# Attention and two mixtures of experts: late tokens of one expert chosen by a product with ones and zeros, list reads on another queue, gathers at another place

## The chip, the cores and the metric

The kernel runs on one core of one Trainium2 chip. The metric is the device time of one launch in microseconds: 1219.24 us is the median of 3 runs of the kernel before (1219.02 to 1221.35).

## The reference

Three layers follow each other. The first is causal attention with a decay, over 2 batches, 8 heads, 576 positions and 64 columns a head; its output is a matrix x of N = 1152 tokens by D = 512. The second is a mixture in which every token goes through all E = 8 experts (F = 1024), weighted by a matrix P that eight rounds of normalising make. The third sends each token to the two experts with its highest noisy logits. Cut to the last layer, which the change touches:

```python
def _moe2_ref(x, w_gate, w_noise, noise, w1, w2):
    noisy = x @ w_gate + np.log1p(np.exp(x @ w_noise)) * noise
    top2 = np.argpartition(-noisy, 2, axis=1)[:, :2]
    top2_w = softmax of the two values of each token
    for e in range(E):
        for k in range(2):
            mask = top2[:, k] == e
            h = np.maximum(x[mask] @ w1[e], 0.0)
            out[mask] += top2_w[mask, k, None] * (h @ w2[e])
```

## The kernel before

All large products are split: each f32 operand is stored as a high part and the rest (`xh` and `xl`, `w1h` and `w1l`, `hth` and `htl`), and three matmuls stand for one product. A step of a first product is L205 to L207, of a second product L641 to L643. Weights come from memory in pieces of 512 KB into four `raw` buffers (`load_w`, SyncE's queue, L180 for w1 and L183 for w2). `conv_w` turns a piece into its two parts, with a cast on ScalarE (L200) and a subtraction on VectorE (L201).

The first mixture works through units of 256 or 384 tokens. Its last two experts are ordered so that the first 896 tokens (early) are finished before the last 256 (late). While the late tokens are still in the first mixture, the early ones are already routed for the second. Routing ranks the eight logits of each token on VectorE (`route_rank`, `route_places`), finds for each of its two experts the next free place in that expert's list, and scatters (token number, weight) to `table_scratch` in memory (L969, GpSimd). A place is a row of the table; expert 0 has two lists, list 0 for early tokens and list 1 for late ones, and experts 1 to 7 make lists 2 to 8, worked through in the order of their lengths (`order_lists`, `by_length`, and `pick`, which loads an expert's number into a register of SyncE, L1018).

A list l goes through these steps. `read_list(l)` loads its part of the table into `tb` (L988, SyncE's queue) and makes clipped indices `ix` (L989, VectorE). `gather_x(l)` fetches the rows of x with one indirect DMA for each 128 places or fewer (L1030, GpSimd) into a part of `acc`, one of two halves by turns (`xsl[l % 2]`). `turn_x(l)` transposes them on TensorE (L1044) and makes `xh` and `xl` with a copy on ScalarE (L1046) and a subtraction on VectorE (L1047). `m2_g1(l)` is the first product and its ReLU. List 1 has its own form with the tokens as the fixed operand: L1058 to L1060, a ReLU on ScalarE (L1062), four transposes (L1065), and `hth` and `htl` from ScalarE (L1068) and VectorE (L1069). `m2_g2(l)` is the second product, with a gather of what `out` holds by now (L1076) for l above 1. The result is scaled and scattered to `out` (L1110 and L1113 on VectorE, L1114 on GpSimd). Its TensorE accumulators are the `y` buffers, of which there are three.

The passage from the first to the second mixture is written out in `last_units`. Each piece of work gets a planned time, the pieces are sorted by it, and called in that order. The pieces of `T_ROUTE`, `T_CONV` and `T_TURN` are offsets in us from the end of a second product; a step of a second product counts 3 x (512/2400 + 0.0026). `T_TURN` places `turn_x(0)` inside the second product of the unit `i0 + 4`. `early_done` reads and gathers list 0; `late_done`, after the late routing, orders the lists, loads the first weight piece, reads and gathers lists 1 and 2, picks lists 3 to 8 and loads three more pieces. After `last_units` come list 0's second product, list 1's turn and first product, the reads of lists 3 to 8, list 3's gather, list 2's turn, and then the loop over lists 2 to 8, in which list l + 1 is turned in the middle of list l's second product.

Outside blocks with a manual schedule the order of instructions on an engine need not be that of the source: a scheduler places each by its own estimate of readiness. Matmuls in `pin` keep their place behind what was traced before them on TensorE. Each engine then runs its queue in order.

Of the kernel before, what the change touches and what calls it, by code (L numbers as in the profile page):

```python
# [10 lines left out]
F32 = mybir.dt.float32  # L11
F32R = mybir.dt.float32r
BF = mybir.dt.bfloat16
I32 = mybir.dt.int32
# [39 lines left out]
T_ROUTE = [[1.45, 1.8, 3.0, 5.75, 11.65, 0.4, 4.2], [2.0, 3.7, 4.0, 5.9, 6.85, 2.15, 5.55], [1.05, 1.6, 2.65, 6.2, 7.4, 0.4, 3.9], [1.0, 1.15, 2.3, 5.4, 7.15, 3.5, 0.6]]  # L54

T_CONV = [[-1.1, 0.7], [-4.5, 1.65], [2.95, 4.35], [13.6, 2.75]]
T_TURN = 5.75

class Plan:

# [65 lines left out]
def attn_moe_moe2_kernel(ctx: ExitStack, tc: tile.TileContext, q, k, v, f, wg1, w1, w2,  # L126
# [702 lines left out]
    for l in range(E + 1):  # L829
        for t in range(extra[l]):  # L830
            nc.gpsimd.memset(limit[:, l, t:t + 1], float((base[l] if l == 1 else 0) + caps[l] + t * 128))
    number = mp.tile([1, E], F32, name="number")
    for e in range(E):
        nc.gpsimd.memset(number[:, e:e + 1], float(e))
# [105 lines left out]
    def route_places(t0, t1):  # L940
        n = t1 - t0
        rk, nl, kbf = RT.pop("rank")
        pr = RT.pop("pr")
        km = mp.tile([128, 2, 3, E], F32, name="r_km")[:, :, 0:n]
        for z in range(2):
            nc.vector.tensor_scalar(km[:, z], rk, float(z), None, op0=OP.is_equal)
        kw = mp.tile([128, 2, 3, E], F32, name="r_kw")[:, :, 0:n]
        m12 = mp.tile([128, 2, 3], F32, name="r_m12")[:, :, 0:n]
        nc.vector.tensor_tensor(kw, km, nl[:, None].to_broadcast([128, 2, n, E]), op=OP.mult)
        nc.vector.tensor_reduce(m12, kw, axis=AX.X, op=OP.add)  # L950
        ex = mp.tile([128, 3], F32, name="r_ex")[:, 0:n]
        nc.vector.tensor_tensor(ex, m12[:, 1], m12[:, 0], op=OP.subtract)
        nc.scalar.activation(ex, ex, AF.Exp)
        pos = mp.tile([128, 3, E], F32, name="r_pos")[:, 0:n]
        nc.vector.tensor_tensor(pos, pr[:, 0:n * E].rearrange("p (t e) -> p t e", e=E),
                                nxt[:, None, :].to_broadcast([128, n, E]), op=OP.add)
        nc.vector.tensor_tensor(nxt, nxt, pr[:, 64:64 + E], op=OP.add)
        nc.vector.tensor_tensor(kw, km, pos[:, None].to_broadcast([128, 2, n, E]), op=OP.mult)
        pf = mp.tile([128, 2, 3], F32, name="r_pf")[:, :, 0:n]
        nc.vector.tensor_reduce(pf, kw, axis=AX.X, op=OP.add)  # L960
        nc.vector.tensor_copy(place[:, :, t0:t1], pf)  # L961
        sm = mp.tile([128, 3], F32, name="r_sm")[:, 0:n]
        wr = rows.bitcast(F32)[:, t0:t1]
        nc.vector.tensor_scalar(sm, ex, 1.0, 1e-9, op0=OP.add, op1=OP.add)
        nc.vector.reciprocal(wr[:, :, 0, 1], sm)
        nc.vector.tensor_tensor(wr[:, :, 1, 1], ex, wr[:, :, 0, 1], op=OP.mult)
        for t in range(t0, t1):
            for z in range(2):
                s = nc.gpsimd.indirect_dma_start(  # L969
                    out=table, out_offset=bass.IndirectOffsetOnAxis(ap=place[:, z, t:t + 1], axis=0),  # L970
                    in_=rows[:, t, z, :], in_offset=None)
                for o in scat:
                    tc.declare_no_dep(s.ins, o.ins, reason="each list entry has one writer")
                scat.append(s)

    tabs, idxs = {}, {}

    def read_list(l):

        nt = -(-caps[l] // 128)  # L980
        st = caps[l] // nt
        tb = mp.tile([st, nt, 2], I32, name=f"tb{l}")
        ix = mp.tile([st, nt], I32, name=f"ix{l}")
        if l < 2:
            src = table[base[l]:base[l] + caps[l], :]
        else:
            src = table[ds(by_length[l - 2] * room + (base[2] - room), caps[l]), :]
        nc.sync.dma_start(tb, src.rearrange("(s t) c -> s t c", t=nt))  # L988
        nc.vector.tensor_scalar(ix, tb[:, :, 0], float((NT - TC if l == 0 else NT) - 1), None, op0=OP.min)  # L989
        tabs[l], idxs[l] = tb, ix  # L990

    def order_lists():

# [32 lines left out]
    def gather_x(l):  # L1026
        ix = idxs[l]
        st = ix.shape[0]
        for t in range(ix.shape[1]):
            nc.gpsimd.indirect_dma_start(  # L1030
                out=xsl[l % 2][0:st, t, :], out_offset=None, in_=x2d[0:NT - TC] if l == 0 else x2d,
                in_offset=bass.IndirectOffsetOnAxis(ap=ix[:, t:t + 1], axis=0))

    def cols(l):
        c = xcol[l % 2]
        return xh[:, :, c.start:c.start + caps[l]], xl[:, :, c.start:c.start + caps[l]]

    def turn_x(l):
        st, nt = idxs[l].shape
        ah, al = cols(l)  # L1040
        for kc in range(KC):
# [3 lines left out]
                                        ident[0:st, 0:st]))  # L1045
            nc.scalar.copy(ah[:, kc], pt[:, :caps[l]])  # L1046
            nc.vector.tensor_tensor(al[:, kc], pt[:, :caps[l]], ah[:, kc].bitcast(F32), op=OP.subtract)  # L1047

    def m2_g1(l, ht, fcs=range(FC)):
        ah, al = cols(l)  # L1050
# [79 lines left out]
    def last_units(i0):  # L1130
# [88 lines left out]
        def late_done():  # L1219
# [2 lines left out]
            pick(2)  # L1222
            load_w(E + 1, 0, (0,))
            read_list(1)
            gather_x(1)
            read_list(2)
            gather_x(2)
            for l in range(3, E + 1):
                pick(l)
            load_w(E + 1, 0, (1, 2, 3))  # L1230

        now = unit(0, i0 + 1)
        now, ends = back(now, i0)
# [25 lines left out]
    for i, (s, e, c0, n) in enumerate(units[:hi - 5]):  # L1259
# [7 lines left out]
        if units[i + 1][0] != s:  # L1267
            conv_next(s + 1, 1)
    last_units(hi - 5)
    m2_g2(0, hts[hi % 2])  # L1270
    turn_x(1)
    m2_g1(1, hts[(hi + 1) % 2])

    for l in range(3, E + 1):
        read_list(l)
    gather_x(3)
    turn_x(2)
    s = E + 1
    conv_next(s + 1, 0)
    m2_g2(1, hts[(hi + 1) % 2])  # L1280
    conv_next(s + 1, 1)
    for l in range(2, E + 1):
# [4 lines left out]
        m2_g1(l, ht, range(2, FC))  # L1287
        s = E + l
        if l < E:
            if l > 2:  # L1290
                gather_x(l + 1)
            conv_next(s + 1, 0)
        m2_g2(l, ht, (lambda: turn_x(l + 1)) if l < E else None)
        if l < E:
            conv_next(s + 1, 1)

# [83 lines left out]
```

## Time and profile before

| | |
|---|---|
| runs, median | 1219.24 us |
| profiled execution, time | 1218.53 us |
| its span, first to last instruction | 1216.5 us |
| mean granted TensorE clock | 0.991 |
| TensorE busy (matmul) | 1180.1 us, 97% |
| VectorE, ScalarE, GpSimd busy | 521.7, 381.3, 196.8 us |
| memory moved | 100.90 MB, mean 83 GB/s |

The span is what the trace shows; the time has some 2 us around it. TensorE's busy share is that of matmuls in flight. The granted clock is a share of 2.4 GHz; 0.50 is the level of 1.2 GHz. A wait in brackets is idle time of the engine ahead of the instruction, with the instruction or transfer that ended it.

### The profile page before, as it was taken

How to read it: one execution, taken by the hardware profiler on the slowest of the kernel's cores; microseconds unless marked ns; L12 is line 12 of the kernel's file. 1: busy time of each engine (PE TensorE's matmuls, PEld its weight loads, DVE VectorE, ACT ScalarE, POOL GpSimd, SP SyncE). 2: the span in 40 equal slices, each digit the busy share in tenths (PEclk: the TensorE clock that was granted, in tenths of full speed). 3: DMA queues.
4: the chain of work that ended last, by engine and by line, in shares of the span. 5: the costliest groups of instructions: out<-in, count | busy, mean ns of one | idle time of the engine just before them, and what ended most of it. 6: DMA issues, size and time to landing. Idle time of an engine off the chain costs nothing. (4 is left out here: it accounts for less than half of the span.)

```text
span 1216.5 us, 17348 instructions
## 1 busy us (share of the span) xinstructions
PE 1180.1 (97%) x6949; PEld 1090.1 (90%) x6949; DVE 521.7 (43%) x1042; ACT 381.3 (31%) x725; POOL 196.8 (16%) x273
## 2 busy tenths in 40 slices
PE   7999999999999999999999999999999969999996
PEld 6899989999999999999999999998897959999995
DVE  5887565232232332313323223223455646556541
ACT  4787522122121221212212112212133335444440
POOL 4854500000000000000000000000112143443232
PEclk9999999999999999999999999999999989999998
DMA  5541142021120201202102112012032368676632
GB/s 135 141 88 41 46 150 70 1 70 35 35 70 1 70 18 52 70 1 70 60 10 70 33 37 70 32 39 79 27 96 85 107 197 238 200 225 215 185 89 62
DMA packets 104041, 100.90 MB, mean 83 GB/s; under 512 B 44798, under 2 KB 79742, under 8 KB 103951
## 3 DMA queue, kind: packets, MB, share of 16 engines
q1 hardware_dynamic: 90799, 85.44, 23.2%
q0 software_dynamic: 13152, 14.27, 4.2%
q8 instruction: 56, 0.92, 0.3%
q14 instruction: 34, 0.28, 0.1%
HBM read 90.05 MB, written 9.98 MB: 82 GB/s over the span
## 5 line engine op out<-in xcount | busy, mean ns | idle before, releaser
L205 PE MATMUL h<-xh,w1h 128*128 128x384 f32 (+8 forms) x1056 | 336.4, 319 | 1.0 <-DVE htl L636 1.0
L207 PE MATMUL h<-xh,w1l 128*128 128x384 f32 (+8 forms) x1056 | 334.3, 317 | 0.0
L206 PE MATMUL h<-xl,w1h 128*128 128x384 f32 (+8 forms) x1056 | 334.2, 317 | 0.0
L635 ACT ACTIVATE hth<-h 128x384 fp32r<-128x384 f32 (+8 forms) x264 | 119.3, 454 | 477.8 <-PE h L207 477.7
L643 PE MATMUL y<-w2h,htl 128*128 128x512 f32 (+1 forms) x624 | 244.4, 392 | 8.1 <-DVE htl L1069 8.1
L641 PE MATMUL y<-w2h,hth 128*128 128x512 f32 (+1 forms) x624 | 244.9, 392 | 0.0
L642 PE MATMUL y<-w2l,hth 128*128 128x512 f32 (+1 forms) x624 | 244.1, 391 | 0.0
L636 DVE SCALAR_TENSOR_TENSOR htl<-h,hth 128x384 fp32r<-128x384 f32 (+8 forms) x264 | 132.7, 508 | 186.6 <-ACT hth L635 186.3
L205 PEld LDWEIGHTS h<-xh,w1h 128*128 128x128 f32 x1056 | 199.3, 189 | 2.9 <-DVE htl L636 1.5
L206 PEld LDWEIGHTS h<-xl,w1h 128*128 128x128 f32 x1056 | 199.3, 189 | 1.0
L207 PEld LDWEIGHTS h<-xh,w1l 128*128 128x128 f32 x1056 | 199.3, 189 | 0.0
L643 PEld LDWEIGHTS y<-w2h,htl 128*128 128x128 f32 (+1 forms) x624 | 117.3, 188 | 33.6 <-DVE htl L1069 8.6
L969 POOL DMA_INDIRECT table_scratch<-rows,place x18 | 17.5, 974 | 785.9 <-DVE place L961 722.7
L641 PEld LDWEIGHTS y<-w2h,hth 128*128 128x128 f32 (+1 forms) x624 | 117.4, 188 | 23.8
L642 PEld LDWEIGHTS y<-w2l,hth 128*128 128x128 f32 (+1 forms) x624 | 117.4, 188 | 23.8
L787 DVE SCALAR_TENSOR_TENSOR acc<-y,Pgate,acc 128x512 f32<-128x512 f32 x52 | 39.0, 750 | 201.7 <-PE y L643 201.7
L201 DVE TENSOR_TENSOR w1l<-raw,w1h 128x1024 fp32r<-128x1024 f32 x64 | 78.1, 1223 | 70.1 <-ACT w1h L200 70.1
L200 ACT CAST w2h<-raw 128x1024 fp32r<-128x1024 f32 x68 | 70.2, 1050 | 94.8 <-PE y L643 91.2
L201 DVE TENSOR_TENSOR w2l<-raw,w2h 128x1024 fp32r<-128x1024 f32 x68 | 81.0, 1220 | 38.0 <-ACT w2h L200 35.9
L200 ACT CAST w1h<-raw 128x1024 fp32r<-128x1024 f32 x64 | 67.2, 1050 | 80.6 <-PE h L206 56.2
L1087 PE MATMUL y<-hth,w2h 128*128 128x282 f32 (+5 forms) x192 | 58.1, 302 | 0.0
L1089 PE MATMUL y<-htl,w2h 128*128 128x282 f32 (+5 forms) x192 | 57.6, 300 | 0.0
(252 smaller groups left out, 1200.4 us busy)
## 6 DMA issues: line engine op xcount, KB each, us to landing
raw<-in_moe_w_dram SPq DMA_DIRECT2D x136, 512.0 KB, 4.1
out_dram<-zer SPq DMA_DIRECT2D x1, 2304.0 KB, 7.9
x_scratch<-acc SPq DMA_DIRECT2D x9, 256.0 KB, 2.6
raw_q<-in_q_dram SPq DMA_DIRECT2D x16, 128.0 KB, 2.6
raw_k<-in_k_dram SPq DMA_DIRECT2D x16, 128.0 KB, 2.6
raw_v<-in_v_dram SPq DMA_DIRECT2D x16, 128.0 KB, 2.7
cl<-ncum_scratch SPq DMA_DIRECT2D x14, 144.0 KB, 2.9
acc<-x_scratch,ix POOLq DMA_INDIRECT x24, 5.4
```

The costliest lines, as they stand in the source:

```text
L200: nc.scalar.copy(hv, rv)
L201: nc.vector.tensor_tensor(lv, rv, hv.bitcast(F32), op=OP.subtract)
L205: nc.tensor.matmul(pt[:, :n], w1h[:, kc, fs], ah[:, kc, :], start=kc == 0, stop=False)
L206: nc.tensor.matmul(pt[:, :n], w1h[:, kc, fs], al[:, kc, :], start=False, stop=False)
L207: nc.tensor.matmul(pt[:, :n], w1l[:, kc, fs], ah[:, kc, :], start=False, stop=kc == KC - 1)
L635: nc.scalar.activation(hh[:, fc, :n], pt[:, :n], AF.Relu)
L636: nc.vector.scalar_tensor_tensor(hl[:, fc, :n], pt[:, :n], 0.0, hh[:, fc, :n].bitcast(F32), op0=OP.max, op1=OP.subtract)
L641: nc.tensor.matmul(py[:m], hh[:, fc, ts], w2h[:, fc, :], start=fc == 0, stop=False)
L642: nc.tensor.matmul(py[:m], hh[:, fc, ts], w2l[:, fc, :], start=False, stop=False)
L643: nc.tensor.matmul(py[:m], hl[:, fc, ts], w2h[:, fc, :], start=False, stop=fc == FC - 1)
L1087: nc.tensor.matmul(py[:, :caps[l]], w2h[:, fc, dsl], ht[0][:, fc, :caps[l]], start=fc == 0, stop=False)
L1089: nc.tensor.matmul(py[:, :caps[l]], w2h[:, fc, dsl], ht[1][:, fc, :caps[l]], start=False, stop=fc == FC - 1)
```

## The change

`T_TURN` goes from 5.75 to 9.2. List 1 is no longer gathered and turned: VectorE makes, for each of the two late token tiles, a 128 by 128 matrix with a one where the token's place equals the column's place number, and `choose_x` multiplies the late tokens, which are still in `acc`, with it on TensorE, which gives x of list 1 with tokens in columns. List 1's table part is still read for its weights and token numbers, without indices. Tables of lists 3 to 8 are read on ScalarE's queue, with their expert's number loaded to a register of ScalarE; the reads stand ahead of list 0's second product in the source. The three weight pieces of `late_done` are issued ahead of the picks of lists 3 to 8. List 3 is gathered after list 1's first product as before, list 4 now behind list 2's turn, and list l + 3 behind the turn of list l + 1.

```diff
--- before.py
+++ after.py
@@ -54,7 +54,7 @@
 T_ROUTE = [[1.45, 1.8, 3.0, 5.75, 11.65, 0.4, 4.2], [2.0, 3.7, 4.0, 5.9, 6.85, 2.15, 5.55], [1.05, 1.6, 2.65, 6.2, 7.4, 0.4, 3.9], [1.0, 1.15, 2.3, 5.4, 7.15, 3.5, 0.6]]
 
 T_CONV = [[-1.1, 0.7], [-4.5, 1.65], [2.95, 4.35], [13.6, 2.75]]
-T_TURN = 5.75
+T_TURN = 9.2
 
 class Plan:
 
@@ -829,6 +829,12 @@
     for l in range(E + 1):
         for t in range(extra[l]):
             nc.gpsimd.memset(limit[:, l, t:t + 1], float((base[l] if l == 1 else 0) + caps[l] + t * 128))
+
+    slots = mp.tile([128, caps[1]], F32, name="slots")
+    chosen = mp.tile([128, TC // 128, caps[1]], F32, name="chosen")
+    slot_i = chosen[:, 0, :].bitcast(I32)
+    nc.gpsimd.iota(slot_i, pattern=[[1, caps[1]]], base=base[1], channel_multiplier=0)
+    nc.gpsimd.tensor_copy(slots, slot_i)
     number = mp.tile([1, E], F32, name="number")
     for e in range(E):
         nc.gpsimd.memset(number[:, e:e + 1], float(e))
@@ -972,6 +978,11 @@
                 for o in scat:
                     tc.declare_no_dep(s.ins, o.ins, reason="each list entry has one writer")
                 scat.append(s)
+        if t1 == NTT:
+            at0 = mp.tile([128, 3], F32, name="r_at0")[:, 0:n]
+            nc.vector.tensor_tensor(at0, kw[:, 0, :, 0], kw[:, 1, :, 0], op=OP.add)
+            for t in range(n):
+                nc.vector.tensor_scalar(chosen[:, t, :], slots, at0[:, t:t + 1], None, op0=OP.is_equal)
 
     tabs, idxs = {}, {}
 
@@ -984,10 +995,15 @@
         if l < 2:
             src = table[base[l]:base[l] + caps[l], :]
         else:
-            src = table[ds(by_length[l - 2] * room + (base[2] - room), caps[l]), :]
-        nc.sync.dma_start(tb, src.rearrange("(s t) c -> s t c", t=nt))
-        nc.vector.tensor_scalar(ix, tb[:, :, 0], float((NT - TC if l == 0 else NT) - 1), None, op0=OP.min)
+            at = by_length[l - 2] if l == 2 else nc.values_load(
+                RT["by"][0:1, l - 2:l - 1], engines=[mybir.EngineType.Activation], min_val=1, max_val=E - 1)
+            src = table[ds(at * room + (base[2] - room), caps[l]), :]
+
+        eng = nc.sync if l < 3 else nc.scalar
+        eng.dma_start(tb, src.rearrange("(s t) c -> s t c", t=nt))
         tabs[l], idxs[l] = tb, ix
+        if l != 1:
+            nc.vector.tensor_scalar(ix, tb[:, :, 0], float((NT - TC if l == 0 else NT) - 1), None, op0=OP.min)
 
     def order_lists():
 
@@ -1031,6 +1047,11 @@
                 out=xsl[l % 2][0:st, t, :], out_offset=None, in_=x2d[0:NT - TC] if l == 0 else x2d,
                 in_offset=bass.IndirectOffsetOnAxis(ap=ix[:, t:t + 1], axis=0))
 
+    def next_x(l):
+        turn_x(l + 1)
+        if l + 3 <= E:
+            gather_x(l + 3)
+
     def cols(l):
         c = xcol[l % 2]
         return xh[:, :, c.start:c.start + caps[l]], xl[:, :, c.start:c.start + caps[l]]
@@ -1045,6 +1066,20 @@
                                         ident[0:st, 0:st]))
             nc.scalar.copy(ah[:, kc], pt[:, :caps[l]])
             nc.vector.tensor_tensor(al[:, kc], pt[:, :caps[l]], ah[:, kc].bitcast(F32), op=OP.subtract)
+
+    def choose_x():
+
+        ah, al = cols(1)
+        pt = ps.tile([128, 512], F32, name="h", bufs=4)
+        n = TC // 128
+        for kc in range(KC):
+            for t in range(n):
+                pin(nc.tensor.matmul(pt[:, kc * 128:kc * 128 + caps[1]],
+                                     acc[:, NTT - n + t, kc * 128:kc * 128 + 128], chosen[:, t, :],
+                                     start=t == 0, stop=t == n - 1))
+        pv = pt.rearrange("p (k x) -> p k x", k=KC)[:, :, 0:caps[1]]
+        nc.scalar.copy(ah, pv)
+        nc.vector.tensor_tensor(al, pv, ah.bitcast(F32), op=OP.subtract)
 
     def m2_g1(l, ht, fcs=range(FC)):
         ah, al = cols(l)
@@ -1222,12 +1257,11 @@
             pick(2)
             load_w(E + 1, 0, (0,))
             read_list(1)
-            gather_x(1)
             read_list(2)
             gather_x(2)
+            load_w(E + 1, 0, (1, 2, 3))
             for l in range(3, E + 1):
                 pick(l)
-            load_w(E + 1, 0, (1, 2, 3))
 
         now = unit(0, i0 + 1)
         now, ends = back(now, i0)
@@ -1267,14 +1301,15 @@
         if units[i + 1][0] != s:
             conv_next(s + 1, 1)
     last_units(hi - 5)
-    m2_g2(0, hts[hi % 2])
-    turn_x(1)
-    m2_g1(1, hts[(hi + 1) % 2])
-
+    choose_x()
     for l in range(3, E + 1):
         read_list(l)
+    m2_g2(0, hts[hi % 2])
+    m2_g1(1, hts[(hi + 1) % 2])
+
     gather_x(3)
     turn_x(2)
+    gather_x(4)
     s = E + 1
     conv_next(s + 1, 0)
     m2_g2(1, hts[(hi + 1) % 2])
@@ -1287,10 +1322,8 @@
         m2_g1(l, ht, range(2, FC))
         s = E + l
         if l < E:
-            if l > 2:
-                gather_x(l + 1)
             conv_next(s + 1, 0)
-        m2_g2(l, ht, (lambda: turn_x(l + 1)) if l < E else None)
+        m2_g2(l, ht, (lambda: next_x(l)) if l < E else None)
         if l < E:
             conv_next(s + 1, 1)
```

## Rows read from the trace of the kernel before

**Rows 1.** Two stages: us; busy by engine; granted clock; DMA share; GB/s

```profile
940.00:1002.00 62.00, 49.02 (x275) 42.38 (x275) 32.99 (x92) 23.50 (x43) 17.04 (x15) 0.89 0.53 157
...
1002.00:1207.00 205.00, 204.03 (x1465) 199.13 (x1463) 106.12 (x152) 87.38 (x154) 72.90 (x55) 1.00 0.61 181
```

**Rows 2.** Timeline of TensorE: start, us, instruction, idle before it, releaser

```profile
939.82 0.27 PE L1044 MATMUL h<-ident,acc 128*128 128x128 f32 x1
...
942.89 1.74 PE L1044 MATMUL h<-ident,acc 128*128 128x128 f32 x7 [2.81 <-DMA acc<-x_scratch,ix]
...
950.58 0.28 PE L205 MATMUL h<-xh,w1h 128*128 128x256 f32 x1
...
964.50 0.40 PE L641 MATMUL y<-w2h,hth 128*128 128x512 f32 x1
...
977.57 0.66 PE L1044 MATMUL h<-ident,acc 128*128 128x128 f32 x4 [2.00 <-DMA acc<-x_scratch,ix]
...
978.26 0.50 PE L1058 MATMUL y<-w1h,xh 128*128 128x512 f32 x1
...
993.18 0.80 PE L643 MATMUL y<-w2h,htl 128*128 128x512 f32 x1 [8.14 <-DVE htl L1069]
```

**Rows 3.** Short stretches after the two longer waits, columns as in rows 1

```profile
943.00:944.00 1.00, 1.00 (x6) 1.00 (x6) 1.00 (x2) 0.33 (x1) 0.00 (x0) 0.50 1.00 356
...
994.00:996.00 2.00, 2.00 (x12) 1.81 (x11) 1.48 (x3) 0.71 (x2) 1.04 (x1) 0.50 0.79 303
...
996.00:998.00 2.00, 2.00 (x10) 1.73 (x9) 1.68 (x4) 1.87 (x5) 0.00 (x0) 0.61 1.02 257
```

**Rows 4.** Timeline of SyncE's queue: start, us until the last is issued

```profile
971.62 0.91 SPq L988 DMA_DIRECT2D tb<-table_scratch  x2
...
976.78 1.66 SPq L180 DMA_DIRECT2D raw<-in_moe_w_dram  x3
...
978.67 9.77 SPq L988 DMA_DIRECT2D tb<-table_scratch  x6
```

**Rows 5.** The chain of waits, 960 to 1002: start, us, what

```profile
966.18 5.36 DMA table_scratch<-rows,place
...
978.67 11.61 DMA tb<-table_scratch
...
990.30 0.17 DVE ix L989
```

**Rows 6.** Waits of SyncE's queue, 984 to 987: us, times, longest

```profile
SPq L988 <- DMA raw<-in_moe_w_dram: 0.9, 1, 0.9
```

**Rows 7.** Timeline of ScalarE, columns as in rows 2

```profile
944.26 1.05 ACT L200 CAST w1h<-raw 128x1024 fp32r<-128x1024 f32 x1 [0.93 <-DMA raw<-in_moe_w_dram]
...
947.61 1.06 ACT L200 CAST w2h<-raw 128x1024 fp32r<-128x1024 f32 x1 [0.26 <-PE y L643]
...
950.57 2.00 ACT L200 CAST w2h<-raw 128x1024 fp32r<-128x1024 f32 x2
...
985.84 1.04 ACT L200 CAST w1h<-raw 128x1024 fp32r<-128x1024 f32 x1 [2.46 <-DMA raw<-in_moe_w_dram]
```

**Rows 8.** Timeline of VectorE, columns as in rows 2

```profile
945.34 1.23 DVE L201 TENSOR_TENSOR w1l<-raw,w1h 128x1024 fp32r<-128x1024 f32 x1 [0.60 <-ACT w1h L200]
...
961.32 0.19 DVE L958 TENSOR_TENSOR r_kw<-r_km,r_pos 128x32 f32<-128x32 f32 x1
...
973.38 0.15 DVE L989 TENSOR_SCALAR ix<-tb 128x1 int32<-128x1 int32 x1 [7.32 <-DMA tb<-table_scratch]
```

**Rows 9.** Line L1030 at 977.4: duration ns; us from issue to landing

```profile
L1030 POOL DMA_INDIRECT acc<-x_scratch,ix x1: 1469/1469/1469, 977.4 to 977.4; - x1
...
DMA to landing us min/median/max: 11.8/11.8/11.8
```

**Rows 10.** Timeline of TensorE, true f32 products, columns as in rows 2

```profile
7.65 2.28 PE L289 MATMUL t<-xf,P 16*128 16x288 f32 x4
...
951.30 0.96 PE L879 MATMUL m<-wgn,yt 128*128 128x16 f32 x8
```

## The prediction

> **What bounds the kernel now.** The first view to read is the table of stages. From 1002 to 1207 us TensorE is busy 204.03 of 205 us; only less work would shorten that stretch, and the change takes none out of it. Between 940 and 1002 TensorE is busy 49.02 of 62 us, at a mean granted clock of 0.89 [rows 1]. This is the passage from the first mixture to the second, and nearly all that the diff touches lies in it.
>
> The second view is TensorE's own order of instructions there, with the idle time before each [rows 2]. Three waits make up the 13 us. At 939.82 the turn of list 0 (L1044) begins and then stands 2.81 us for a gather, until 942.89. At 977.57 the turn of list 1 has stood 2.00 us for its gather. At 993.18 the second product of list 1 has stood 8.14 us for htl, L1069 on VectorE. The third view is the clock: after the first wait it is 0.50 (the 1.2 GHz level) in three slices of 1 us, 943 to 946, of which the first is shown; after the third the same in 992 to 996, whose second half is shown, and 0.61 to 998 [rows 3]. So the first wait costs 2.81 + 3 x 0.5 = 4.3 us. The third costs 8.14, plus half of the 2.82 us from 993.18 to 996, plus 0.39 x 2: 10.3 us. The second left the clock up and costs 2.0.
>
> The fourth view says what the 8.14 us is. The chain of waits runs through a table read, issued at 978.67, that took 11.61 us until the first ix (L989) at 990.30 [rows 5]. On SyncE's queue six such reads stand behind three weight loads of 512 KB issued from 976.78 [rows 4]; VectorE takes its instructions in order, and six L989 stand ahead of L1069. The loads in turn stand behind six register loads (L1018), which lie between the two reads that end at 972.53 and the loads: 4.25 us, 0.7 each [rows 4].
>
> **A, T_TURN 5.75 to 9.2.** One step of a return product (three matmuls) is planned at 3 x (512/2400 + 0.0026) = 0.648, so the turn now comes after 15 of the 16 steps rather than 9: 18 matmuls later. The 48 of list 0 fill 964.50 to 975.57 (977.57 less its wait), 0.23 each, so TensorE arrives 4.1 us later, at 943.9. The gather was there at 942.89. That wait goes with 1.0 us to spare, as nothing ahead of it changes.
>
> What is late next: the first product of list 0 (L205), now at 950.58, would be reached at 943.9 + 0.8 (eight transposes at 0.1, half of what the seven from 942.89 take at low clock) + 0.7 (three matmuls) + 0.4 (a token tile's four transposes) = 945.8. It needs xh and xl, which ScalarE and VectorE make from the turn. ScalarE was then converting weights, 1.05 us a piece: w1's last from 944.26, when its load came, w2's second at 947.61, its last two from 950.57 [rows 7]; VectorE adds 1.23 each, for w1's last until 946.57 [rows 8]. How many conversions of w2 stand ahead of the copies of the turn is open, since engines here don't keep the source's order. None: copies from 945.3, VectorE free at 946.6, L205 at 947.0, a gain of 3.6 at full clock. One: VectorE free at 947.8, L205 at 948.2, a gain of 2.4 less 1.5 for low clock after 2.5 us idle, like the first wait. Two: 950.3 and with low clock a loss of about 1.5. Three: 953.2, a loss of 4.8. I take one, **-0.9**: w2's first piece can be converted as soon as ScalarE ends w1, the second ran only at 947.61. Bounds -4.8 (L205 at 945.8) and +4.8.
>
> **B, list 1 by ones and zeros.** Out go the gather of list 1 and four transposes: the 2.00 us wait and 0.69 us (977.57 to 978.26). In come eight true f32 products of 128 columns. The trace shows such a product as two records. With sixteen columns a record takes (0.96 - 0.25)/7 = 0.10 us, 0.25 being one record's own length; with 288 columns, at the start of the kernel, (2.28 - 0.68)/3 = 0.53, or 0.24 per 128 columns [rows 10]. Sixteen records cost 1.6 to 3.8 us; I take 0.12 each, 1.9, near the lower row as the clock is up here. VectorE gets three instructions of about 0.2 us once kw is there (L958, 961.32 [rows 8]); TensorE reaches the choice at 964.50, so it waits for nothing with some 2 us of cover, or up to 1 us if the chain of order_lists goes first. That chain, and the first weight load after it, slip 0.6 us: covered, as the load is converted after 980. ScalarE's copy and VectorE's subtraction of 512 columns (about 0.6 and 0.7) lie beside m2_g2(0), 11 us long. One gather fewer ahead of list 2's on GpSimd: taken as nothing. Sum **-0.8**, bounds -1.1 and +2.1.
>
> **C, list reads.** SyncE now issues reads 1 and 2 (971.62, when the scatters have landed [rows 4, 5]) and at once the three loads, 4.2 us earlier; the six register loads follow, with nothing urgent behind them. ScalarE loads its own six registers and issues six reads. No row shows a DMA issued by ScalarE; the nearest are SyncE's: 0.91 us for two undisturbed reads and 0.7 for a register, so 2.7 us without the registers and 6.9 with them. The other end is SyncE's 9.77 us for six, swollen by its full queue, plus 4.25: 14.0. ScalarE is done with them between 974.2 and 985.5. Behind them on it stand the ReLUs of list 1, list 2's weight conversions and turn 2's copies. On this axis TensorE ends list 0 at 964.50 + 1.9 + 11.1 = 977.5 and list 1's first product, 6.1 us (978.26 to 984.4, two matmuls before the third wait), at 983.6. Its first ReLU is due at 980.5, its first L1069 at 982.5. ScalarE is free 2 to 6 us before, or late by 5.
>
> The reads land 1.8 us after issue when all is quiet (971.62, ix at 973.38 [rows 8]), 11.6 behind loads. The last may also wait for a load: SyncE's last list read stood 0.9 us for one, just before 986 [rows 6], and a load came to ScalarE's conversion at 985.84 [rows 7]. So the last read lands between 976 and 989 with ScalarE undisturbed, and L1069 and the outputs of list 0 (which hold a y buffer) wait 0 to 6.5 us beyond need. I take 2.5, nearer the quiet end as the loads start only 1 us before the reads, and no fall of the clock, as after the 2.00. The 10.3 us then gives **-7.8**; bounds -10.3 and +4.9 (rival 3).
>
> After that, w1 of list 2 is loaded 4 us earlier and converted once list 1 has read w1h, so its feed keeps pace with an earlier list 2. **The later gathers** move a list further ahead. No turn after 1000 waits for one now, so 0; the same bytes move, and behind GpSimd's gather, which now waits for the turn, stand only the scatters of the next list.
>
> **Sum.** -0.9 - 0.8 - 7.8 = -9.5. The profiled run took 1218.53 (span 1216.5, 2.0 around it): 1209.0. The median of 1219.24 lies 0.7 above: 1209.7, rounded to **1210**.
>
> **Rivals.**
> 1. Everything goes: no conversion delays xh, the reads land in time. 4.8 + 0.8 + 10.3 = 15.9, 1203. For it: the small reads leave the queue that held them. Against: A needs xh within 1.8 us of the turn's arrival.
> 2. The list reads are as late as the loads, queue or no queue. A gather on GpSimd's queue, issued at 977.4, took 11.8 us [rows 9] beside the loads that SyncE's reads waited for. Then the last read lands at 989 and the wait is 5.5 us plus 2 of low clock: 10.3 - 7.5 = 2.8; with A and B 4.5, so 1215. Against: the loads begin 4 us earlier, and the gather of list 1 is gone. The Trainium skill, DMA: Bandwidth & Descriptors (Issuing engines are not separate DMA queues), says that transfers issued by different engines run on the same 16 DMA engines and interleave, and that only issue time is saved. By that rule this rival holds; the gather's 11.8 us agrees with it.
> 3. Slower: ScalarE itself becomes the block, its reads standing ahead of list 1's ReLUs. If its issues are held as SyncE's were (14.0 us, to 985.5) and the last read takes 11.6, VectorE is free at 997 and TensorE waits 13 + 2.2 rather than 10.3: +4.9; with A at two pieces (+1.5) and B -0.8 about +5.6, 1225. It decides from a last landing at about 993. For it: the in-order queue. Against: SyncE's issues were slowed by its own loads ahead of them.
> 4. The moved turn eats what the rest gives: A at +4.8, B, and C as in rival 2: +1.2, 1220, no change.
>
> **How the numbers follow.** Forecast 0.52 (own range 1206 to 1213), rival 1 0.22, rival 2 0.13, rival 3 0.08, rival 4 0.05. The range 1202 to 1217 leaves out rivals 3 and 4 and tails. A change within 0.2% (2.4 us) can't be told from none here: 0.04, most of rival 4; faster 0.88, the forecast, rivals 1 and 2 and a bit of 4; slower 0.08, rival 3.
>
> **What would show it.** A: the turn's wait below 0.3 us, and a new wait of L205 near 946 to 948. B: no L1044 ahead of list 1, sixteen f32 records near 0.12 us each. C: L1069 no longer behind a list read with 8 us of TensorE idle. The stretch that is now 940 to 1002 is shorter by about 9, what follows keeps its 205. I am wrong if TensorE waits more than 5 us in the passage at one place, or if a wait opens after list 2 begins.

## The result: 0.5% slower, and the profile after

The changed kernel takes 1227.09 us (median of 6 runs, 1224.96 to 1228.53) against 1220.3 (6 runs) of the kernel before on the same chip: the ratio is 1.0053, interval [1.0042, 1.0064], some 6.5 us slower. The forecast was 1210, with 1202 to 1217 as its range. The profiled execution took 1228.47 us (span 1226.5).

Line numbers have moved: turn_x is L1065 (copies L1067, L1068), the late tile's transposes L857, the list read L1003 with its index L1006, the gather L1046, the choice L1077 (copies L1081, L1082), list 1's first product L1093 to L1095, its ReLU L1097, its transposes L1100, htl L1104, the outputs L1145 and L1149.

First the stages (columns as in [rows 1]). TensorE is busy 2 us less in the second stretch than before. In the first it is as busy as before, at a lower clock (0.86 against 0.89). List 2 begins only within the second stretch:

```profile
940.00:1002.00 62.00, 49.95 (x264) 43.48 (x262) 30.39 (x86) 18.89 (x33) 14.19 (x12) 0.86 0.50 145
...
1002.00:1207.00 205.00, 201.74 (x1450) 198.16 (x1451) 109.08 (x156) 92.11 (x161) 73.34 (x54) 0.98 0.61 182
```

TensorE's timeline (columns as in [rows 2]) has the places. The turn of list 0 no longer waits, but the four transposes behind it do. The choice runs where it should. Then there are four more waits, and the first product of list 2 (the 128x282 one) comes at 1011.85:

```profile
945.86 1.03 PE L1065 MATMUL h<-ident,acc 128*128 128x128 f32 x8
...
951.83 1.12 PE L857 MATMUL h<-ident,acc 128*128 128x128 f32 x4 [4.24 <-DVE xl L1068]
...
970.65 1.95 PE L1077 MATMUL h<-chosen,acc 128*128 128x128 f32 x16
972.36 0.48 PE L641 MATMUL y<-w2h,hth 128*128 128x512 f32 x1
...
989.94 0.80 PE L1093 MATMUL y<-w1h,xh 128*128 128x512 f32 x1 [3.69 <-DVE acc L1145]
...
997.91 0.30 PE L1065 MATMUL h<-ident,acc 94*128 94x94 f32 x1 [0.64 <-DMA acc<-x_scratch,ix]
...
1000.59 0.30 PE L1065 MATMUL h<-ident,acc 94*128 94x94 f32 x1 [2.37 <-DMA acc<-x_scratch,ix]
...
1003.99 1.36 PE L1065 MATMUL h<-ident,acc 94*128 94x94 f32 x7 [3.10 <-DMA acc<-x_scratch,ix]
...
1011.85 0.29 PE L205 MATMUL h<-xh,w1h 128*128 128x282 f32 x1
```

The traces here come to the passage up to 1.9 us apart, so absolute times of two traces should not be subtracted. I measure from one event that all of them have, the conversion of w2 on ScalarE that waited 6.44 us for L643: the anchor. From it to the first product of list 2 is "the passage" below: 72.05 us before (929.82 to 1001.87), 80.12 after (931.73 to 1011.85). From list 2's first product to the last L643, "the rest" below, it is 204.77 before and 204.90 after. So the passage alone lost the time, 8.07 us of it in these two executions.

Where in the passage, as differences of those rows: to the end of list 0's first product 34.68 us before [rows 2], 38.92 after, +4.24 (A). From there to list 0's second product one has nothing before and 1.71 after; ahead of list 1, before, 2.69 (the wait of 2.00 and 0.69 of transposes), now none: -0.98 (B). List 0's second product is 11.07 and 11.01. From list 1's start to list 2's first product 23.61 before and 28.48 after (983.37 to 1011.85), +4.87 (C).

**Step A.** ScalarE's and VectorE's timelines at the turn (columns as in [rows 7] and [rows 8]):

```profile
946.21 1.05 ACT L200 CAST w1h<-raw 128x1024 fp32r<-128x1024 f32 x1 [0.97 <-DMA raw<-in_moe_w_dram]
947.61 1.04 ACT L200 CAST w2h<-raw 128x1024 fp32r<-128x1024 f32 x1 [0.35 <-PE y L643]
949.14 1.04 ACT L200 CAST w2h<-raw 128x1024 fp32r<-128x1024 f32 x1 [0.48 <-DMA raw<-in_moe_w_dram]
950.09 1.19 ACT L1067 CAST xh<-h 128x256 fp32r<-128x256 f32 x4
```

```profile
948.69 1.23 DVE L201 TENSOR_TENSOR w2l<-raw,w2h 128x1024 fp32r<-128x1024 f32 x1 [0.17 <-ACT w2h L200]
950.22 1.22 DVE L201 TENSOR_TENSOR w2l<-raw,w2h 128x1024 fp32r<-128x1024 f32 x1 [0.30 <-ACT w2h L200]
951.36 1.41 DVE L1068 TENSOR_TENSOR xl<-h,xh 128x256 fp32r<-128x256 f32 x4
```

Two conversions of w2 stand between the turn (ended at 946.9) and its copies. The turn has taken all four `h` buffers (the accumulators of transposes and first products), and L857 needs one, which only the first xl gives back: hence the 4.24 us. The clock then fell and stayed low for about ten microseconds (columns as in [rows 1], of a longer row of such slices the second and the last low ones):

```profile
952.00:954.00 2.00, 2.00 (x10) 2.00 (x11) 2.00 (x5) 1.67 (x3) 0.00 (x0) 0.50 0.28 109
...
960.00:962.00 2.00, 2.00 (x14) 2.00 (x14) 0.61 (x2) 0.38 (x1) 0.00 (x0) 0.70 0.00 0
```

**Step C.** The queues of SyncE and ScalarE (columns as in [rows 4]). Reads 1 and 2, then the loads on SyncE; the six later reads on ScalarE, which took 10.06 us from the first issue to the end of the last, with ScalarE's ReLU of list 1 behind them. Of the 10.06 us the six issues are 5.4 (2.75, 0.59, 0.54, 0.52, 0.49 and 0.55); what is left lies between them, mostly the loading of the experts' numbers to registers (L998):

```profile
979.09 0.92 SPq L1003 DMA_DIRECT2D tb<-table_scratch  x2
980.58 2.31 SPq L180 DMA_DIRECT2D raw<-in_moe_w_dram  x3
```

```profile
979.53 10.06 ACTq L1003 DMA_DIRECT2D tb<-table_scratch  x6
989.63 0.60 ACT L1097 ACTIVATE yt<-y 128x512 f32<-128x512 f32 x1 [14.19 <-DMA tb<-table_scratch]
```

VectorE's order. The shapes tell the lists: 94x3 is list 2, 96x3 list 3, 98x3 list 4. Here list 3's index is the first instruction, and list 2's only comes within the pair of 988.38; an output (L1145), which gives a `y` buffer back to list 1's first product, comes behind five indices:

```profile
986.26 0.17 DVE L1006 TENSOR_SCALAR ix<-tb 96x3 int32<-96x3 int32 x1 [10.09 <-DMA tb<-table_scratch]
988.38 0.30 DVE L1006 TENSOR_SCALAR ix<-tb 98x3 int32<-98x3 int32 x2 [1.96 <-DMA tb<-table_scratch]
988.99 0.41 DVE L1006 TENSOR_SCALAR ix<-tb 100x3 int32<-100x3 int32 x2 [0.31 <-DMA tb<-table_scratch]
989.14 0.74 DVE L1145 TENSOR_SCALAR acc<-y,tb 128x512 f32<-128x512 f32 x1
...
991.65 0.17 DVE L1006 TENSOR_SCALAR ix<-tb 110x3 int32<-110x3 int32 x1 [1.70 <-DMA tb<-table_scratch]
```

GpSimd's order. The gathers of 0.95 and 0.93 us are two of list 3's three; list 2's three, with 1.5 to 1.7 us each, stand behind them:

```profile
987.23 0.95 POOL L1046 DMA_INDIRECT acc<-x_scratch,ix  x1 [13.28 <-PE y L1095]
988.49 0.93 POOL L1046 DMA_INDIRECT acc<-x_scratch,ix  x1 [0.30 <-issue]
989.72 1.49 POOL L1046 DMA_INDIRECT acc<-x_scratch,ix  x1 [0.30 <-issue]
...
993.30 1.66 POOL L1046 DMA_INDIRECT acc<-x_scratch,ix  x1 [0.30 <-issue]
```

The chain of waits (columns as in [rows 5]) runs through it: scatter, ScalarE's first issue, the read of list 4 (its index is the first of the pair), list 2's index, its last gather, and TensorE:

```profile
973.00 5.95 DMA table_scratch<-rows,place
...
979.53 2.75 ACTq L1003
...
983.07 4.96 DMA tb<-table_scratch
...
988.38 0.31 DVE ix L1006 x2
...
993.30 10.64 DMA acc<-x_scratch,ix
1003.99 1.36 PE h L1065 x7
```

So it is another list's read that held list 2's index. In e6 below, where that index stands ahead of those of the later lists, it comes 3.4 us after SyncE began to issue reads 1 and 2 (974.34 to 977.70), in the changed kernel with that order (e13) 3.0 us; here it comes 9.3 us after (979.09 to 988.38). The rows of e6, SyncE's queue and VectorE:

```profile
974.34 0.92 SPq L1003 DMA_DIRECT2D tb<-table_scratch  x2
```

```profile
977.70 0.17 DVE L1006 TENSOR_SCALAR ix<-tb 94x3 int32<-94x3 int32 x1 [7.36 <-DMA tb<-table_scratch]
```

### The profile page after: what moved, and what is told of

The parts are those of the page before. It is cut to its first block, busy times and chain, and to the rows that moved or that the text cites. A ratio compares the mean times of both kernels' runs of the same rounds, so it can differ in the third digit from the quotient of the medians.

```text
span 1226.5 us, 17396 instructions
## 1 busy us (share of the span) xinstructions
PE 1188.7 (97%) x6961; PEld 1098.2 (90%) x6961; DVE 522.4 (43%) x1041; ACT 381.2 (31%) x722; POOL 198.5 (16%) x274
## 5 line engine op out<-in xcount | busy, mean ns | idle before, releaser
L205 PE MATMUL h<-xh,w1h 128*128 128x384 f32 (+8 forms) x1056 | 337.3, 319 | 1.3 <-DVE htl L636 1.3
L643 PE MATMUL y<-w2h,htl 128*128 128x512 f32 (+1 forms) x624 | 244.1, 391 | 0.0
L205 PEld LDWEIGHTS h<-xh,w1h 128*128 128x128 f32 x1056 | 200.4, 190 | 3.1 <-DVE htl L636 1.7
L643 PEld LDWEIGHTS y<-w2h,htl 128*128 128x128 f32 (+1 forms) x624 | 117.2, 188 | 24.9
```

The lines of the kernel that those rows point to most:

```text
L205: nc.tensor.matmul(pt[:, :n], w1h[:, kc, fs], ah[:, kc, :], start=kc == 0, stop=False)
L643: nc.tensor.matmul(py[:m], hl[:, fc, ts], w2h[:, fc, :], start=False, stop=fc == FC - 1)
```

## The experiments

My theory after the result had two independent causes: the moved turn (two conversions and the four `h` buffers), and the order of the lists' indices on VectorE, which decides more than the queue that reads them. The rivals were that the reads' queue or the shared DMA engines set the time, and that ScalarE was blocked by its own issues.

| kernel | ratio, 95% interval | passage, us | rest, us |
|---|---|---|---|
| before | 1 | 72.05 | 204.77 |
| changed | 1.0053 [1.0042, 1.0064] | 80.12 | 204.90 |
| e1 changed, turn back | 1.0016 [1.0004, 1.0028] | 75.05 | 204.63 |
| e2 A alone | 1.0051 [1.0033, 1.0068] | 76.73 | 205.44 |
| e3 B alone | 0.999 [0.998, 1.0] | 71.26 | 205.23 |
| e4 C alone | 0.9985 [0.9974, 0.9996] | 71.34 | 211.81 |
| e5 e1, loads behind the picks | 0.9979 [0.9967, 0.9991] | 72.11 | 205.85 |
| e6 e1, indices late | 0.9966 [0.9951, 0.9981] | 66.77 | 210.52 |
| e7 e5 and e6 | 0.9976 [0.9963, 0.9989] | 65.78 | 210.78 |
| e8 B, indices late | 1.0321 [1.0303, 1.034] | 67.47 | 253.48 |
| e10 e6, T_TURN 7.9 | 0.9966 [0.9952, 0.998] | 64.71 | 212.06 |
| e11 before, indices behind list 1 | 0.9977 [0.9959, 0.9996] | 66.08 | 209.41 |
| e12 e11 and B | 0.9969 [0.9954, 0.9984] | 67.08 | 212.45 |
| e13 changed, indices late | 1.0009 [0.9994, 1.0023] | 70.58 | 212.90 |

The ratio comes from 5 to 12 runs of each kernel against 13 to 29 of the kernel before on the same chip (6 against 6 for the changed kernel); the passage and the rest come from one profiled execution each.

**e1, the changed kernel with the turn back**

```diff
-T_TURN = 9.2
+T_TURN = 5.75
```

> The changed kernel with T_TURN back at 5.75. Theory (two losses add: the moved turn, and the order of the list reads' indices on VectorE): the 4.24 us wait of the late tile's transposes (L857) for xl goes and the gather wait of 2.8 us comes back; 4 to 5 us less than the changed kernel, about 1222. Rival (the reads on ScalarE are the whole loss): within 1 us of the changed kernel's 1227.

Measured: 0.37% less than the changed kernel, and a passage 5.07 us shorter, but not the kernel before: waits of 9.7 us for gathers (2.64 of them list 0's, as before) and 2.5 for `y` stay. So with B and C in place A costs 4.5 of the 6.5 us, and B and C together still lost 3 us of passage.

**e2, A alone**

```diff
-T_TURN = 5.75
+T_TURN = 9.2
```

> The kernel before with T_TURN 9.2 and nothing else. Theory: the late tile's transposes wait about 4 us for an h buffer behind two w2 conversions, and list 0 ends 4 us later: about 1224. As the prediction had it (one conversion ahead): 0.9 us less, 1219.

Measured: with nothing else changed the ratio is that of the whole change, and the passage is 4.68 us longer. TensorE's timeline shows the wait at the same place and of the same size:

```profile
950.17 0.67 PE L851 MATMUL h<-ident,acc 128*128 128x128 f32 x4 [3.96 <-DVE xl L1047]
```

**e3, B alone, and e4, C alone**

```diff
-            gather_x(1)
...
+    choose_x()
...
-    turn_x(1)
```

> The kernel before with list 1 chosen by ones and zeros and nothing else: SyncE reads all lists, loads and gathers as before. Theory: the 2.0 us wait of list 1's turn goes, sixteen records cost 1.7, the 8 us wait of L643 stays in full: 0 to 2 us less than before, about 1219. Rival (the choice itself costs): 2 us more or worse.

```diff
+        eng = nc.sync if l < 3 else nc.scalar
+        eng.dma_start(tb, src.rearrange("(s t) c -> s t c", t=nt))
...
+            load_w(E + 1, 0, (1, 2, 3))
             for l in range(3, E + 1):
                 pick(l)
-            load_w(E + 1, 0, (1, 2, 3))
```

> The kernel before with lists 3 to 8 read on ScalarE's queue ahead of list 0's second product and the three loads ahead of the picks; T_TURN 5.75, list 1 gathered. VectorE's order puts the indices of lists 3 and 4 ahead of those of lists 1 and 2. Theory: the 8.1 us wait goes, and waits for the gathers of lists 1 and 2 and for a y buffer take its place: 2 to 7 us more than before. As the prediction had it: 7.8 us less. Rival (ScalarE held by the reads): its ReLU of list 1 is the releaser of TensorE's wait.

Measured: each gains 0.7 to 0.8 us of passage, about a tenth of a per cent. In e3 TensorE came earlier to the same wait, 10.4 us at L643 rather than 8.14. In e4 that wait is gone, as the prediction had it, and another of the same size stands ahead of it, because list 1's index now waits on VectorE behind other indices. The 2 to 7 us more that I expected of e4 did not come: its time is 0.15% less. Its wait ends with a gather, not with ScalarE's ReLU, so the rival had the wrong releaser:

```profile
985.16 1.12 PE L1047 MATMUL h<-ident,acc 128*128 128x128 f32 x4 [9.47 <-DMA acc<-x_scratch,ix]
```

**e5, loads behind the picks again (on e1)**

```diff
             gather_x(2)
-            load_w(E + 1, 0, (1, 2, 3))
             for l in range(3, E + 1):
                 pick(l)
+            load_w(E + 1, 0, (1, 2, 3))
```

> e1_turn_back with the three weight loads behind the picks again, so that the reads on ScalarE start some 4 us ahead of them. Theory (the order of indices on VectorE and of gathers on GpSimd, list 3's ahead of list 2's): waits for list 2's gather and a y buffer shrink only in part, 0 to 3 us less than e1 (1221 to 1224). Rival (the loads slow the small reads and the gathers): both waits nearly go, 6 us less or better (1218).

Measured: list 2's gather is in time (list 0's takes 2.28), but `y` waits 9.1 us for L1145, which has index instructions ahead of it. Better than e1 by 0.37%, some 4.5 us and so between the two forecasts, and still a stall of 9 us: the order of the queues moves the stall, and does not remove it.

**e6, the indices of lists 3 to 8 made at each list's gather (on e1), and e7, the same on e5**

```diff
-        if l != 1:
+        if l != 1 and l < 3:
             nc.vector.tensor_scalar(ix, ...
...
+        if l > 2:
+            pin(nc.vector.tensor_scalar(ix, tabs[l][:, :, 0], float(NT - 1), None, op0=OP.min))
```

> e1_turn_back with the indices of lists 3 to 8 made only at each list's gather, pinned behind what is traced before; the reads stay on ScalarE. Theory (order of indices): list 2's gather goes out before list 3's, the y wait of 2.5 us goes, the wait of list 2's turn falls from 9.7 to 4 us or less: 6 to 9 us less than e1, about 1217. Rival (loads and reads share the DMA engines): 0 to 3 us less.

> e6 and e5 together. Theory: about e6, perhaps 1 to 2 us less, 1215 to 1217. Rival: as e5, 1218.

Measured: the passage falls to 66.77 and 65.78 us; against e1 no read is moved, and the waits for `y` and for list 2's gather are gone. The time of e7 is no less than that of e6 (the intervals overlap), so its expected 1 to 2 us did not show. What is left in e6 is the gather of list 0 (3.0) and 3.6 us for the ReLU on ScalarE, whose six reads take 11.25 us with the register loads between them:

```profile
974.78 11.25 ACTq L1003 DMA_DIRECT2D tb<-table_scratch  x6
986.07 0.60 ACT L1099 ACTIVATE yt<-y 128x512 f32<-128x512 f32 x1 [16.45 <-DMA acc<-x_scratch,ix]
```

Only 4.1 us of e6's 5.3 show in the median. Its profiled execution, which was its slowest (1220.46), has 3.6 us of a new wait near 1095, in list 5's first product: list 5's ReLUs stand on ScalarE behind the conversion of list 6's first piece of w1, which waits for its load. From the anchor, that load went out 3.9 us earlier than before (150.56 against 154.42) and took 11.16 us rather than 8.23, so it landed only 0.9 us earlier, where list 2 had begun 5.3 us earlier. It is the same pattern once more, an in-order engine that waits for data of a later list ahead of work that is ready. The chain of e6:

```profile
1081.61 11.16 DMA raw<-in_moe_w_dram
...
1092.87 1.04 ACT w1h L200
...
1094.80 0.40 PE h L205
```

**e8, B with the indices late (on e3)**

```diff
-        if l != 1:
+        if l != 1 and l < 3:
...
+        if l > 2:
+            pin(nc.vector.tensor_scalar(ix, tabs[l][:, :, 0], float(NT - 1), None, op0=OP.min))
...
-    gather_x(3)
     turn_x(2)
+    gather_x(3)
```

> e3_choose_only (lists read on SyncE, behind the loads) with the indices of lists 3 to 8 made at each list's gather and list 3's gather behind list 2's turn. Theory (VectorE's order, not the queue of the reads, holds L643): the 8 to 10 us wait of L643 goes with no read moved, list 2's gather costs up to 3: 7 us less than e3, about 1214. Rival (the reads' queue): as e3, 1220.

Measured: a miss. The passage is 4.6 us shorter than before, but the whole 3.2% longer: TensorE waits 37.0 us in 10 places for gathers after 1000 us. A gather whose index is made at its place (L1044 here) goes out on GpSimd behind those that fetch an output's parts (L1107), which wait for the output's scatters:

```profile
1047.28 0.94 POOL L1107 DMA_INDIRECT acc<-out_dram,ix  x1 [11.44 <-DMA out_dram<-acc,tb]
...
1050.99 0.98 POOL L1044 DMA_INDIRECT acc<-x_scratch,ix  x1 [0.30 <-issue]
```

In e6, where each gather stands further ahead in the source, there is no such wait: an index made at its gather needs the change's place for the gathers. The two differ in the reads' queue as well, but e12 below rules that out: it has the reads on SyncE's queue and the gathers of lists 4 to 8 where e8 has them, makes the indices right behind list 1, and waits for no gather after list 2 has begun.

**e10, the turn of list 0 between the two places (on e6)**

```diff
-T_TURN = 5.75
+T_TURN = 7.9
```

> The changed kernel with the indices of lists 3 to 8 made late (as in the kernel that pins each list's index at its gather), and T_TURN 7.9: the turn of list 0 stands four steps of the return product later than with 5.75 and two earlier than with 9.2, so that one conversion of w2, not two, stands ahead of its copies. With 5.75 TensorE waited 3.0 us for list 0's gather, ratio 0.9966. Theory (what A costs is the second conversion ahead of the copies): the wait for the gather falls to 0.3 to 1.0, the late tile's transposes wait under 1.5 us for xl, passage 64 to 66 us (from 66.8), 1215 to 1217, ratio 0.995. Rival (any later turn costs, since all four h buffers are taken so much later): the late tile waits 3 us or more, passage 68 or more, ratio 0.999 or above.

Measured: between the two. One conversion stands ahead of the copies. The wait for the gather is gone (0.17), but L857 waits 3.00, as ScalarE begins w1's last piece only at 945.46, when its load has come:

```profile
944.15 0.99 PE L1067 MATMUL h<-ident,acc 128*128 128x128 f32 x7 [0.17 <-DMA acc<-x_scratch,ix]
...
949.53 0.66 PE L857 MATMUL h<-ident,acc 128*128 128x128 f32 x4 [3.00 <-DVE xl L1070]
```

The clock stayed at 1.00 from 940 to 960, and the passage is 2.06 us shorter than e6's, but the time is the same. So not every later turn costs, as the rival had it; but the second conversion isn't the whole cost either, since with one the late tile waits as long as the gather did.

**e11, the kernel before with the six indices behind both L1069 of list 1**

```diff
-        nc.vector.tensor_scalar(ix, tb[:, :, 0], float((NT - TC if l == 0 else NT) - 1), None, op0=OP.min)
+        if l < 3:
+            nc.vector.tensor_scalar(ix, ...
...
     for l in range(3, E + 1):
         read_list(l)
+        pin(nc.vector.tensor_scalar(idxs[l], tabs[l][:, :, 0], float(NT - 1), None, op0=OP.min))
```

> The kernel before with one thing changed: the six indices L989 of lists 3 to 8 stand on VectorE behind both L1069 of list 1 rather than ahead of them; their reads stay where they were on SyncE's queue. Theory (the wait of 8.1 us at L643 is a matter of VectorE's order, not of the queue of the reads): htl no longer waits for the last read but for the first piece of list 2's w1, which came to ScalarE at 985.84, so VectorE is free at about 988.3; L643 waits 2.5 to 4.5 us, the passage is 4 to 5 us shorter (67 to 68), 1216 to 1218 with some of it given back later, ratio 0.996 to 0.998. Rival (the reads' queue is the cause, as the prediction had it): L643 waits 7 us or more still, or the same time comes back at list 2's gather; ratio 0.999 to 1.001.

Measured: the 8.14 us at L643 are gone altogether, with the reads where they were, 9.55 us in SyncE's queue behind three loads. SyncE's and VectorE's timelines of e11:

```profile
979.23 9.55 SPq L988 DMA_DIRECT2D tb<-table_scratch  x6
```

```profile
986.90 0.68 DVE L1070 TENSOR_TENSOR htl<-h,hth 128x512 fp32r<-128x512 f32 x1
...
990.69 0.68 DVE L1070 TENSOR_TENSOR htl<-h,hth 128x512 fp32r<-128x512 f32 x1
991.29 0.32 DVE L1277 TENSOR_SCALAR ix<-tb 96x3 int32<-96x3 int32 x2
...
992.64 0.17 DVE L1277 TENSOR_SCALAR ix<-tb 110x3 int32<-110x3 int32 x1 [0.29 <-DMA tb<-table_scratch]
```

This settles what the wait was: the reads come no earlier, and nobody needs them then. The passage is 6.0 us shorter; 7.9 us of waits for gathers remain, among them list 1's 3.8, and the median gain is 2.8 us.

**e12, e11 with B**

```diff
-            gather_x(1)
...
+    choose_x()
...
+        pin(nc.vector.tensor_scalar(idxs[l], tabs[l][:, :, 0], float(NT - 1), None, op0=OP.min))
```

> The kernel before with two things changed: list 1 chosen by ones and zeros (B of the prediction), and the six indices of lists 3 to 8 on VectorE behind both L1069 of list 1 (its own numbering: L1098). T_TURN is 5.75, the reads of lists 3 to 8 stay on SyncE's queue behind the weight loads. With the order alone the passage was 66.1 us and TensorE then waited 3.8 us for list 1's gather and 1.9 for list 2's. Theory (the reads' queue does not matter once the indices stand behind list 1's work): list 1's gather is gone, its 3.8 us less about 1.3 for the choice's products, so the passage is 63 to 65.5 us; the wait for list 2's gather stays under 2; 1215 to 1218, ratio 0.994 to 0.997, with part of the passage's gain lost again after 1000 us at the weight conversions. Rival (with list 1 earlier, the reads of SyncE's queue or the weight load behind them become the limit again): L643's successor or list 2's gather waits 4 us or more, passage 66 or more, ratio 0.998 or above.

Measured: the ratio is the theory's, the passage the rival's. Nothing waits for the gathers of lists 1 and 2, but list 1's second ReLU (L1091 in its numbering) stands on ScalarE behind a conversion that waits 5.60 us for its load, as the loads are behind the picks here (978.14):

```profile
987.51 1.04 ACT L200 CAST w1h<-raw 128x1024 fp32r<-128x1024 f32 x1 [5.60 <-DMA raw<-in_moe_w_dram]
988.46 0.59 ACT L1091 ACTIVATE yt<-y 128x512 f32<-128x512 f32 x1
```

So the other half of C, loads ahead of the picks, might have a use here. That version, with the reads left on SyncE, was not tried, and it is not shown.

**e13, the changed kernel with the indices late**

```diff
-        if l != 1:
+        if l != 1 and l < 3:
...
+        if l > 2:
+            pin(nc.vector.tensor_scalar(ix, tabs[l][:, :, 0], float(NT - 1), None, op0=OP.min))
```

> The changed kernel as it is (T_TURN 9.2), with the indices of lists 3 to 8 made late. The order of VectorE's and GpSimd's work on the lists is mended, the turn is not. Theory (two causes that add: the turn +4 to +6 in all, the order of the indices the rest): the late tile's transposes still wait 4 us for xl, the waits for y and for list 2's gather (3.7 and 6.1) fall below 2 together; 1221 to 1223, ratio 0.999 to 1.001, that is 3.5 to 5 us above the same kernel with 5.75. Rival (the order of the indices carries the whole loss): 1217 to 1219, ratio 0.997.

Measured: the waits for `y` and list 2's gather are gone, L857 still waits 4.5 and the ReLU 4.2, and the time stands 0.43% above e6's, 5.3 us, with T_TURN the only difference. The two causes add, as the theory had it. Against the changed kernel the turn alone (e1) gives back 4.5 us, the order of the indices alone (e13) 5.4, both (e6) 10.6, close to their sum and more than the loss of 6.5.

The best here are e6 and e10, both 0.34% faster than the kernel before, and e12, e11, e7 and e5 can't be told from them, as the intervals overlap.

## Why the prediction was wrong, step by step

**What bounds the kernel: right, and incomplete.** In the changed kernel the passage decides, and the rest kept its 205. But the third wait, which carried most of the forecast, was read one row too short. The chain [rows 5] names the read ahead of the six indices, and so the read seemed late. The row that mattered was VectorE's order: work that was ready stood behind six instructions that nobody needed before list 3. e11 shows it.

**A failed, -0.9 against +4.24 in the passage.** Two errors. "I take one" conversion ahead of the copies; there were two. And for the case of two the price was put at 1.5, which has the right time of L205 in it and a clock that is much too cheap. L205 was forecast at 950.3 and came at 950.7 on the axis of the trace before (952.60 less the 1.91 between the anchors). The wait stood elsewhere: the late tile's transposes, for which the prediction only counted their 0.4 us, had to wait, as the turn holds every `h` buffer. But the 4.24 of new wait is no more than the 2.81 and the 1.5 of the old one, so L205 begins only 0.1 us later than before. Nearly the whole +4.24 comes behind it: from L205's start to the end of list 0's first product it is 13.92 us before (950.58 to 964.50) and 18.05 after (952.60 to 970.65). The clock is low from about 951 to 961 there, against three slices ahead of L205 before [rows 3]. So low clock, taken as under 2 us after the first wait, cost 4.1. On the whole time A costs 4.5 (the changed kernel against e1) to 6.2 us (e2).

**B was right**, -0.98 against -0.8: no wait for `chosen`, sixteen records in 1.71 us where 1.9 was taken, the wait of 2.00 and 0.69 gone. Alone it bought nothing measurable (e3), since the same wait followed.

**C failed, -7.8 against +4.87.** "L1069 no longer behind a list read with 8 us of TensorE idle" came true. The failing term is the "2.5" for what waits for the last read. It took the order of the source for list 2's index and list 0's outputs, although the text says in A that engines here don't keep it. With the later reads on ScalarE's queue, VectorE got list 3's index ahead of list 2's and of the outputs, and GpSimd list 3's gather ahead of list 2's. The 8.14 and its 2.2 of low clock became 3.69 + 0.64 + 2.37 + 3.10 = 9.80, with two spells at half clock (989 to 995, 1003 to 1009). TensorE works through 5.4 and 5.0 us of these spells, so by estimate they cost 5.2; with the waits that is 4.7 us more than before, nearly all of the +4.87. In e6 and e13 the same reads on the same queue, with the later indices late, bring neither the wait for `y` nor the one for list 2's gather; what is left there is the wait for ScalarE's ReLU, 3.6 and 4.2 us. The prediction's own sign of being wrong, a wait of more than 5 us at one place, did not show: the longest is 4.24, and the waits are spread over five places.

**"The later gathers: 0" failed in the same way**: two of list 3's gathers hold GpSimd for 2.5 us ahead of list 2's (987.23 to 989.72).

**The rivals.** Rival 2 had its mechanism. With the loads behind the picks, the index of list 8, the last read, ran at 991.80, 61.77 us after the anchor, when ScalarE had issued the reads (e5), and at 992.64, 62.17 after it, when SyncE had (e11), though ScalarE's first issue came 5.8 us earlier from the anchor. With the loads ahead of the picks, 3.8 us earlier, it ran at 55.30 after the anchor (e1, reads on ScalarE's queue). So the place of the loads, and not the queue, set when the last read landed. The rule that it cited from the Trainium skill, DMA: Bandwidth & Descriptors (Issuing engines are not separate DMA queues), that transfers interleave on the same 16 DMA engines whoever issues them, agrees with these rows. The same section calls the issue time that is saved usually small beside the transfer. Here issuing was no small thing: the six issues were 5.4 us on ScalarE in the changed kernel and 8.5 on SyncE in e11, a single one up to 2.75 and 3.26; the measurement decides. Rival 3 had the nearest time (1225), and half of its mechanism: ScalarE's issues do hold the ReLU (989.63 after, and 2.9 to 4.2 us of wait in e6, e7, e10 and e13), but in the changed kernel VectorE held TensorE to 989.94 anyway. Rival 4 was near in its step (A eats), yet none had the order of VectorE and GpSimd in it.

**What stays open.** The passage's gains of 5 to 7 us in e6, e7, e10, e11 and e12 became 2.8 to 4.2 us of time. In their profiled executions the rest is 209 to 212 us rather than 205, which takes most or all of the gain back: TensorE waits 4.6 to 5.5 us there for htl ahead of L205, against 1.0 before, where weights come just in time. How much of this the median run has is not settled. The rest can be long without a shorter passage too (211.81 in e4, whose profiled execution was its slowest), and the profiled execution of the kernel before (1218.53) is one of its fastest, as its runs beside the experiments went from 1218.36 to 1227.15.

## What to carry to other kernels

When a wait names a transfer, first ask who needs the data: if an in-order engine waits for it ahead of work that is ready, move the waiting instruction back before you move the transfer. Before pricing a moved step, write down for each engine what will stand directly ahead of and behind it in the built order, which the source doesn't tell, and how many buffers of a ring it takes from its neighbours. Moving issues from SyncE to a compute engine costs that engine the whole time of issuing, register loads included (10.06 us here), and can pay only if nothing urgent stands behind them. And read what stands behind the stage that got shorter: here, in the profiled executions, the rest grew as list 2 began earlier.

## What the hardware showed that was not expected

A small read took 0.33 us to issue on SyncE's queue in the changed kernel, ahead of the three loads of 512 KB, and up to 3.26 in e11, behind them. On ScalarE the first of the six took 2.7 to 3.6 us (e4, e5, e6 and the changed kernel), in e5 too, where the loads went out only 4.9 us after it began, and the other five 0.5 to 0.6 each; why the first is so long is open. And the length of a wait did not tell whether the clock fell: after 2.81 us at [rows 2] it was 0.50 for 3 us, after 3.00 us in e10 it stayed at 1.00, and after 4.24 it was low for ten.
